# A fixed order of steps up to chunk 3, chunk 0's relu outputs kept in DRAM, and early keys and values summed by TensorE

## The chip, the cores and the metric

The kernel runs on one core of a Trainium2 chip. The metric is the device time of one execution, in microseconds (us). TensorE (PE; PEld is its weight load), VectorE (DVE), ScalarE (ACT), GpSimd (POOL) and the DMA queues, most of them issued by SyncE (SP), each work through their own list of instructions in order and wait for each other by semaphores.

## The reference

Attention over keys and values that are averaged in groups of eight along the sequence, then a layer norm, a two-layer network with relu, and the sum of both. The weights come as 64-bit floats, all else as 32-bit.

```python
# q, k, v: 8 batches x 8 heads x 576 rows x 64
k_p = k.reshape(B, H, 72, 8, 64).mean(axis=3)
v_p = v.reshape(B, H, 72, 8, 64).mean(axis=3)
attn = softmax(q @ k_p.T / sqrt(64))
x = (attn @ v_p), heads side by side           # 8 x 576 x 512
xn = (x - mean) / sqrt(var + 1e-6) * g_ln
out = x + relu(xn @ w_ch1) @ w_ch2             # 512 -> 2048 -> 512
```

## The kernel before

The 4608 rows are 36 tiles of 128, and nine chunks of four tiles (0 to 8). A tile goes through two stages. `stage_a` loads the tile's queries, forms the scores with the block-diagonal pooled keys `kblk` (TensorE, L310), takes their maximum and subtracts it (VectorE, L319 and L320), takes the exponential (ScalarE, L329) and transposes the result: the first five tiles (`XT`) by TensorE (L335), copied out by ScalarE (L336), the others by a DMA from a float16 pair `phl` (ScalarE L338, GpSimd L345 and L348, SP L355). `values` multiplies with the pooled values (L392, L394, L395), divides by the sums (VectorE L399 to L409, ScalarE L416), normalises (VectorE L420 to L425 with an iterated inverse square root, L372 and L375; ScalarE L428) and transposes z for the network: by TensorE for the first tiles (L438 to L440), for later ones as a float16 pair and a DMA transpose.

Every float32 matrix product of the network is three products of float16 halves. The first layer of chunks 0 and 1 is `ffn_in` (L625), whose relu goes to a ring tile in two halves, by ScalarE (L633) and VectorE (L634); from chunk 2 on it is `slot`, 28 Strassen products of twelve matmuls (L551). The second layer is `ffn_out` (L655): eight groups of 24 matmuls in a chunk, two for each tile, each evicted by VectorE (L665).

The weights have to be made first. Each of eight blocks of w1 and of w2 (1 MB of 64-bit floats) is loaded, converted to float32 (`convert`: ScalarE L189, VectorE L198 or GpSimd, VectorE L199, ScalarE L207 with the block's maximum), and then split into two float16 parts by `split_w` (ScalarE L164, VectorE L165), once the maxima of four blocks have given the scale. The first half of the first layer needs the four splits of blocks 0 to 3, and the first group of the second layer those of four blocks of w2. `w_forms` prepares sums of w1's blocks for the Strassen products on GpSimd (L510, L513).

Keys and values are pooled in halves of a batch: on VectorE by one reduction (L682, L690), or on GpSimd by three additions (L248 to L252, L260 to L262). Values of batch 0 are summed by TensorE, with a band of ones (L755); its keys by VectorE and GpSimd. From batch 1 on, values are then split into a float16 pair, which four DMAs on ScalarE's queue lay out (L283, L284).

The order is set twice. The table `START` names operations up to the end of chunk 1 (`R.1.2` loads block 2 of w1, `C` converts, `S` splits, `A.4` and `B.4` are the two stages of tile 4, `I.0.2` is the first layer of chunk 0 for relu quarter 2, `O.0.1` the second half of its second layer, `HK` and `HV` are halves of pooling). It is emitted operation by operation, and then a scheduler that simulates a timeline reorders instructions within each engine's list. From chunk 2 on a loop emits 28 products and eight groups of the second layer, numbered 0 to 35, and puts the two stages of the next chunk's tiles ahead of the numbers in `A_AT` and `B_AT`; the same scheduler orders it.

Of the kernel before, what the change touches and what calls it, by code (L numbers as in the profile page):

```python
# [70 lines left out]
def attn_ffn_kernel(ctx: ExitStack, tc: tile.TileContext, qT, vn, kT, v, g, w1, w2, out):  # L71
# [74 lines left out]
    def all_max(src, n=P):  # L146


        e, dst = scalar_tile("rowmax"), scalar_tile("allmax")
# [9 lines left out]
        nc.vector.tensor_reduce(out=dst, in_=ps, axis=AX.X, op=ALU.max)
        return dst  # L160

    def split(src, scale, hi, lo):

        nc.scalar.activation(out=hi, in_=src, func=AF.Copy, scale=scale)  # L164
        nc.vector.scalar_tensor_tensor(  # L165
# [16 lines left out]
    def convert(mat, b, on_pool=0):  # L182
# [6 lines left out]
        nc.scalar.activation(  # L189
            out=w, in_=hi.bitcast(F32), func=AF.Prelu, scale=2.0**-112, alpha=-(2.0**32)  # L190
        )
# [7 lines left out]
        nc.vector.scalar_tensor_tensor(  # L199
            out=w.bitcast(I32),  # L200
            in0=w.bitcast(I32),
# [5 lines left out]
        nc.scalar.activation(  # L207
# [37 lines left out]
    def pool_k(b, p, eng):

        kr = kraw.pop((b, p))
        eng.tensor_add(out=kr[:, 0:4, :], in0=kr[:, 0:4, :], in1=kr[:, 4:8, :])  # L248
# [579 lines left out]
```

## Time and profile before

| | |
|---|---|
| three runs | 858.0, 860.56 and 857.74 us; median 858.0 |
| the profiled execution | 858.18 us, of which the span 856.5 us |
| mean granted clock of TensorE | 0.976 |
| instructions | 14301 |
| last matmul of the second layer, chunk 1, 2, 3 | 255.2, 351.4, 435.6 us |
| the same, chunk 4 to 8 | 520.9, 605.1, 690.35, 774.5, 852.6 us |

The times of the trace count from the start of the span. A row of the timeline gives the start, the length, the engine, the line, the operation with output and inputs, the number of instructions in the row, and in brackets the idle time ahead of it with what ended it. From chunk 3 on a chunk takes 84.2 to 85.3 us; chunk 2 took 96.2 us, and the first two together 255.2 us.

### The profile page before, as it was taken

How to read it: one execution, taken by the hardware profiler on the slowest of the kernel's cores; microseconds unless marked ns; L12 is line 12 of the kernel's file. 1: busy time of each engine (PE TensorE's matmuls, PEld its weight loads, DVE VectorE, ACT ScalarE, POOL GpSimd, SP SyncE). 2: the span in 40 equal slices, each digit the busy share in tenths (PEclk: the TensorE clock that was granted, in tenths of full speed). 3: DMA queues.
4: the chain of work that ended last, by engine and by line, in shares of the span. 5: the costliest groups of instructions: out<-in, count | busy, mean ns of one | idle time of the engine just before them, and what ended most of it. 6: DMA issues, size and time to landing. Idle time of an engine off the chain costs nothing.

```text
span 856.5 us, 14301 instructions
## 1 busy us (share of the span) xinstructions
PE 811.7 (95%) x5601; PEld 526.3 (61%) x5601; DVE 530.3 (62%) x1168; ACT 361.4 (42%) x705; POOL 226.3 (26%) x238
## 2 busy tenths in 40 slices
PE   5587989999998899999999999999999999999998
PEld 3466644444546764796478647954785479548743
DVE  5899899124885588387837853785457545843421
ACT  4788653234334543364335523552354235423300
POOL 2586391992212111121210230113011201220000
PEclk9768999999998999999999999999999999999999
DMA  9978352200747144354334451334133512440001
GB/s 336 363 282 275 81 131 82 75 1 16 159 118 173 49 85 90 99 142 84 83 81 102 103 106 38 88 79 103 38 74 75 99 41 47 63 99 25 1 1 50
DMA packets 142867, 86.39 MB, mean 101 GB/s; under 512 B 121824, under 2 KB 122832, under 8 KB 140752
## 3 DMA queue, kind: packets, MB, share of 16 engines
q1 hardware_dynamic: 141456, 84.43, 38.3%
q10 hardware_dynamic: 1344, 1.05, 0.6%
q8 instruction: 44, 0.72, 0.3%
q14 instruction: 23, 0.19, 0.1%
HBM read 45.09 MB, written 9.44 MB: 64 GB/s over the span
## 4 chain that ended last, share of the span: by engine, by line
PE 74%; DVE 11%; DMA 6%; ACT 3%; POOL 3%; issue 2%; SPq 1%; DVEq 0%; POOLq 0%; ACTq 0%
PE ps_f L655 34%; PE ps_f L551 28%; PE ps_f L625 6%; PE ps L310 3%; DMA vr<-in_v_dram 2%; DVE vp L690 2%; DVE w L165 2%; DMA pt<-phl 2%; DVE w L199 1%; POOL w L510 1%; PE ps L394 1%; DVE kp L682 1%; PE ps L395 1%; DMA kr<-in_kT_dram 1%; DMA zz<-hl 1%
## 5 line engine op out<-in xcount | busy, mean ns | idle before, releaser
L655 PE MATMUL ps_f<-w,ring 128*128 128x512 f16 x1728 | 381.6, 380 | 3.4 <-DVE ring L634 2.0
L655 PEld LDWEIGHTS <-ring 128*128 128x128 f16 x1728 | 167.5, 98 | 199.1 <-issue 5.7
L551 PE MATMUL ps_f<-zz,w 128*128 128x256 f16 x1344 | 164.0, 274 | 6.5 <-DMA zz<-hl 4.5
L551 PEld LDWEIGHTS <-w 128*128 128x128 f16 x1344 | 131.6, 98 | 26.0 <-issue 7.7
L551 PE MATMUL ps_f<-zz,raw 128*128 128x256 f16 x1008 | 121.7, 273 | 1.4 <-DMA zz<-hl 0.8
L345 POOL TENSOR_TENSOR phl<-e,phl 128x512 f16<-128x512 f32 x31 | 37.1, 1195 | 324.7 <-ACT phl L338 315.6
L665 DVE SCALAR_TENSOR_TENSOR x<-ps_f,c_out,x 128x512 f32<-128x512 f32 x72 | 53.5, 745 | 109.6 <-PE ps_f L655 109.6
L551 PEld LDWEIGHTS <-raw 128*128 128x128 f16 x1008 | 98.3, 98 | 14.4 <-issue 2.2
L625 PE MATMUL ps_f<-zz,w 128*128 128x512 f16 (+1 forms) x480 | 89.9, 348 | 6.4 <-DVE ring L634 5.5
L625 PEld LDWEIGHTS <-w 128*128 128x128 f16 x480 | 48.4, 102 | 45.0 <-issue 7.2
L571 DVE SCALAR_TENSOR_TENSOR ring<-ps_f,ring 128x512 f16<-128x512 f32 x56 | 38.4, 685 | 31.2 <-ACT ring L570 31.1
L310 PE MATMUL ps<-kblk,q 128*128 128x144 f32 (+1 forms) x320 | 49.3, 309 | 8.2 <-DVE raw L248 7.7
L582 ACT COPY w<-ps_f 128x512 f32<-128x512 f32 x28 | 16.2, 579 | 93.6 <-PE ps_f L551 93.6
L428 ACT ACTIVATE z<-x,nb,y 128x512 f32<-128x512 f32 x36 | 29.2, 814 | 54.5 <-DVE nb L425 41.8
L571 DVE SCALAR_TENSOR_TENSOR ring<-v,ring 128x512 f16<-128x512 f32 x56 | 40.7, 728 | 16.2 <-ACT ring L570 15.6
L310 PEld LDWEIGHTS ps<-kblk,q 128*128 128x128 f32 (+1 forms) x320 | 41.7, 195 | 12.6 <-DVE raw L248 7.7
L690 DVE TENSOR_REDUCE vp<-vr 72x64 f32<-72x512 f32 x44 | 44.6, 1025 | 7.4 <-DMA vr<-in_v_dram 7.0
L416 ACT ACTIVATE x<-ps,rs 128x64 f32<-128x64 f32 x144 | 33.3, 313 | 31.5 <-DVE x L409 20.8
L570 ACT ACTIVATE ring<-v 128x512 f16<-128x512 f32 x56 | 35.1, 627 | 20.2 <-DVE v L593 13.1
L634 DVE SCALAR_TENSOR_TENSOR ring<-ps_f,ring 128x512 f16<-128x512 f32 (+1 forms) x40 | 22.4, 579 | 32.8 <-ACT ring L633 32.7
L338 ACT CAST phl<-e 128x1024 f16<-128x1024 f32 x31 | 32.4, 1044 | 20.0 <-DMA pt<-phl 18.5
L329 ACT ACTIVATE e<-e 128x576 f32<-128x576 f32 x36 | 24.6, 683 | 37.0 <-DVE e L320 36.7
(125 smaller groups left out, 932.4 us busy)
## 6 DMA issues: line engine op xcount, KB each, us to landing
raw<-in_w_dram SPq DMA_DIRECT2D x12, 1024.0 KB
q<-in_qT_dram SPq DMA_DIRECT2D x36, 256.0 KB
out_dram<-x SPq DMA_DIRECT2D x36, 256.0 KB
kr<-in_kT_dram SPq DMA_DIRECT2D x29, 288.0 KB
vr<-in_v_dram SPq DMA_DIRECT2D x56, 144.0 KB
ring<-in_w_dram SPq DMA_DIRECT2D x4, 1024.0 KB
raw<-in_vn_dram SPq DMA_DIRECT2D x1, 1024.0 KB
va<-vh ACTq DMA_DIRECT2D x14, 65.0 KB
```

The source lines that it names most:

```text
L310: nc.tensor.matmul(ps[r, p // 2, p % 2 * 2 * KV : (p % 2 + 1) * 2 * KV], lhsT=q[:, p, r], rhs=kblk[b % NKB][:, p, :], start=True, stop=True,)
L338: nc.scalar.copy(out=ph[:, :, :, 0:KA], in_=e[:, :, 0:KA].unsqueeze(1).broadcast_to([P, 2, H, KA]))
L345: nc.gpsimd.tensor_tensor(out=ph[:, 0, :, KA:P], in0=e[:, :, 0:KA], in1=ph[:, 0, :, 0:KA], op=ALU.subtract)
L416: nc.scalar.activation(out=xh[:, 4 + i, :], in_=px[:, 1, i, 0:D], func=AF.Copy, scale=rs[:, 4 + i : 5 + i])
L428: nc.scalar.activation(out=z, in_=x, func=AF.Identity, scale=y, bias=nb)
L551: nc.tensor.matmul(ps[:, j], lhsT=w_form(wb, int(m == 2), k)[:, fs], rhs=z_form(za, int(m == 1), k), start=(first and i == 0 and j == 0), ...
L570: nc.scalar.activation(out=hi, in_=src, func=AF.Relu)
L571: nc.vector.scalar_tensor_tensor(out=lo, in0=src, scalar=0.0, in1=hi, op0=ALU.max, op1=ALU.subtract)
L625: nc.tensor.matmul(ps, lhsT=w[:, part, fs], rhs=zT[:, kz, cols], start=(n == 0), stop=(n == 3 * NKT - 1),)
L655: nc.tensor.matmul(ps, lhsT=h[:, part, i, cols], rhs=w[:, wp, j], start=(n == 0), stop=(n == 3 * NFT // 2 - 1),)
L665: nc.vector.scalar_tensor_tensor(out=x, in0=ps, scalar=c_out[:, half : half + 1], in1=x, op0=ALU.mult, op1=ALU.add)
L690: nc.vector.tensor_reduce(out=vp[b][:, h, 0:D], in_=vraw.pop((b, h)).rearrange("p l d -> p d l"), axis=AX.X, op=ALU.add,)
```

## The change

Line numbers below are those of the changed code where a row has a new number: L208 and L210 are the two halves of a split (before L164 and L165), L236, L246, L248 and L257 the conversion (L189, L198, L199, L207), L698 and L730 the first and second layer (L625, L655), L707 and L709 the relu (L633, L634), L761 and L770 the reductions (L682, L690), L741 the eviction of the second layer (L665).

*A fixed order.* Every operation becomes a generator that gives up control after each step. `START` names a step by naming its operation once more, now up to the end of chunk 2 (`U.2.1.3` is product 3 of group 1), and the table is run inside a manual schedule: on each engine the instructions stand as written. The loop starts at chunk 3, still under the scheduler, with other numbers in `A_AT` and `B_AT`.

*Relu outputs in DRAM.* `X.q` stores relu quarter q of chunk 0 (1 MB) to DRAM and `Y.q` loads it back into a ring tile, both on SP's queue.

*Pooling.* Keys and values of batches 0 and 1 are loaded in natural layout into room that is free then (tiles of w2, z's second half) and summed by TensorE: keys by twenty small matmuls a batch (`pe_k`), copied to `kblk` by ScalarE (L842); values by five (`pe_v`), copied by ScalarE (L853). Values of batch 1 on are still split as before. All other pooling is one reduction on VectorE, over eight neighbouring elements, since k and v are laid out with those innermost; GpSimd pools nothing.

*Conversion.* `convert` may put its intermediate into PSUM.

```diff
-A_AT, B_AT = (6, 13, 20, 26), (28, 29, 30, 31)
+A_AT, B_AT = (12, 20, 28, 30), (27, 29, 31, 33)
 START = """
-LK Q.0 R.1.2 Q.1 R.1.7 LV C.1.2 R.1.1 C.1.1.1 V0 G R.1.0 HK.1.0 K0 Q.2 R.2.0 C.1.0 R.1.5 A.0 R.1.3
...
+Q.0 LK.0 R.1.6 LV.0 Q.1 LV.1 R.1.2 R.2.4 Q.3 R.1.0 G K.0 R.1.3 R.1.5 LK.1 K.0 HV.2.0 HV.2.1 HK.3.1 K.0 R.1.1
...
+I.0.1.1 C.2.1.1 I.0.1.1 I.0.1.1 C.2.5.0.1 I.0.0.1 S.1.7 M2.0 A.4 I.0.0.1 I.0.1.1 S.1.7 M2.0 C.2.5.0.1 I.0.2 X.0
+A.4 M2.0 T.0.0.1 I.0.1.1 S.2.0 A.5 X.1 B.4 I.0.2 S.2.0 A.5 T.0.0.1 I.0.3 B.4 B.4 I.0.2 Y.0 S.2.1 B.4 I.0.2 A.5
...
     def split(src, scale, hi, lo):
         nc.scalar.activation(out=hi, in_=src, func=AF.Copy, scale=scale)
+        yield
         nc.vector.scalar_tensor_tensor(
...
-    def convert(mat, b, on_pool=0):
+    def convert(mat, b, on_pool=0, in_psum=0):
...
-        w = w_f32(mat, b)
+        w = u = w_f32(mat, b)
+        if in_psum:
+            u = ps_2.tile([P, 2, 512], F32, name="ps_2").rearrange("p a n -> p (a n)")
...
-        kraw[b, p] = kr = wk2.tile([P, POOL, KV], F32, name="kr") if kr is None else kr
+        kraw[b, p] = kr = wk2.tile([P, KV, POOL], F32, name="kr")
...
-        vraw[b, h] = vr = wk2.tile([KV, POOL, D], F32, name="vr") if vr is None else vr
+        vraw[b, h] = vr = wk2.tile([KV, D, POOL], F32, name="vr")
...
         nc.vector.tensor_reduce(
-            out=kp, in_=kr.rearrange("p l k -> p k l"), axis=AX.X, op=ALU.add
+            out=kp, in_=kr, axis=AX.X, op=ALU.add
...
+    def spare(i):
+        if i == 3:
+            kr = wk2.tile([P, KV, POOL], F32, name="kr").rearrange("p k l -> p (k l)")
+            return zz[:, 1].rearrange("p k n -> p (k n)").bitcast(F32), kr
+        return (wt[2][:, 3 * i : 3 * i + 3].rearrange("p s a n -> p (s a n)").bitcast(F32),)
...
+    def pe_k(b):
+        ps = ps_f.tile([P, CH], F32, name="ps_f")[:, : NPAIR * KV].rearrange("p (a k) -> p a k", k=KV)
+        for r, x in enumerate(stage.pop(("k", b))):
+            n = x.shape[0]
+            c = slice(r * P // POOL, r * P // POOL + n // POOL)
+            for p in range(NPAIR):
+                nc.tensor.matmul(
+                    ps[:, p, c],
+                    lhsT=x[:, p * P : (p + 1) * P],
+                    rhs=ones[:n, : n // POOL],
+                    start=True,
+                    stop=True,
+                )
+            yield
+        for j in range(2):
+            r, c = slice(j * D, (j + 1) * D), slice(j * KV, (j + 1) * KV)
+            nc.scalar.copy(out=kblk[b % NKB][r, :, c], in_=ps[r])
+
+    def pe_v(b):
         ps = ps_f.tile([P, CH], F32, name="ps_f")[:KV]
+        for r, x in enumerate(stage.pop(("v", b))):
+            w = pool_w[: x.shape[0], D - r * P // POOL :][:, :KV]
+            nc.tensor.matmul(ps, lhsT=w, rhs=x, start=(r == 0), stop=(r == NRT - 1))
+            yield
...
+    def put_h(q):
+        hd[q] = dram.tile([P, 2, FPQ, CH], F16, name=f"hd{q}")
+        nc.sync.dma_start(out=hd[q], in_=hT.pop((0, q)))
+
+    def get_h(q):
+        hT[0, q] = ring_tile()
+        nc.sync.dma_start(out=hT[0, q], in_=hd.pop(q))
...
+    def step(token):
+        if token not in begun:
+            name, *args = token.split(".")
+            begun[token] = iter(ops[name](*map(int, args)) or ())
+        next(begun[token], None)
+
+    with tc.manual_schedule():
+        for token in START.split():
+            step(token)
+
-    for c in range(ST, NRUN):
+    for c in range(ST + 1, NRUN):
...
-        "kT": k.reshape(B, NPAIR, 2, KV, POOL, D).transpose(0, 2, 5, 1, 4, 3).reshape(B, P, NPAIR, POOL, KV),
+        "kT": k.reshape(B, NPAIR, 2, KV, POOL, D).transpose(0, 2, 5, 1, 3, 4).reshape(B, P, NPAIR, KV, POOL),
```

The order moves at three places. The first is ScalarE's list around the last of the four splits that the first layer waits for; before it read (tiles w_85 and raw hold w1, w_86 w2):

```order
L164 ACTIVATE w_85<-w_85,gs 128x1024
L336 COPY pt<-ps_410 72x1024
L189 ACTIVATE w_85<-raw 128x1024
L164 ACTIVATE w_85<-w_85,gs 128x1024
L207 ACTIVATE raw,wm_92<-w_85 128x1024
L189 ACTIVATE w_85<-raw 128x1024
L164 ACTIVATE w_85<-w_85,gs 128x1024
L416 ACTIVATE x<-ps_591,rs 128x64 x4
L207 ACTIVATE raw,wm_92<-w_85 128x1024
L164 ACTIVATE w_85<-w_85,gs 128x1024
```

and now, with w_87 for w1 and w_88 for w2:

```order
L208 ACTIVATE w_87<-w_87,gs 128x1024
L368 ACTIVATE e<-e 128x576
L236 ACTIVATE w_87<-raw 128x1024
L257 ACTIVATE raw,wm_95<-w_88 128x1024
L377 COPY pt<-ps_532 72x1024
L208 ACTIVATE w_87<-w_87,gs 128x1024
L257 ACTIVATE raw,wm_94<-w_87 128x1024
L208 ACTIVATE w_87<-w_87,gs 128x1024
L461 ACTIVATE x<-ps_555,rs 128x64 x4
L368 ACTIVATE e<-e 128x576
L236 ACTIVATE ps_586<-raw 128x1024
L208 ACTIVATE w_87<-w_87,gs 128x1024
```

The four splits stand in twelve rows instead of ten, with two exponentials and one conversion of w2 between them; ahead of them now stand the values of three tiles instead of two, and the split and the laying out of batch 1's values.

The second is SP's list behind the last weight loads, where the relu quarters go out (hd are the DRAM tiles) and come back:

```order
L225 DMA raw<-in_w_dram 128x2048 x4
L873 DMA hd_950<-ring 128x4096
L873 DMA hd_964<-ring 128x4096
L877 DMA ring<-hd_950 128x4096
L398 DMA_TRANSPOSE pt<-phl_105 128x16x128
L877 DMA ring<-hd_964 128x4096
```

Between two quarters stands the transpose (L398, before L355) of the probabilities of tile 5; before, that transpose had only loads ahead of it on SP.

The third is VectorE's list around the splits of w2 that the first group of the second layer waits for. Before, between the second split and the fourth:

```order
L165 SCALAR_TENSOR_TENSOR w_86<-w_86,ws 128x1024
L375 TENSOR_SCALAR y<-a,y 128x1
L634 SCALAR_TENSOR_TENSOR ring<-ps_f,ring 128x512
L372 TENSOR_SCALAR a<-y,ve 128x1
L159 TENSOR_REDUCE allmax<-ps_f 128x1
L690 TENSOR_REDUCE vp<-vr 72x64
L399 TENSOR_SCALAR sm<-ps_1294,cv 128x8
```

and now:

```order
L210 SCALAR_TENSOR_TENSOR w_88<-w_88,ws 128x1024
L357 TENSOR_REDUCE mx<-ps_1057 128x8
L246 TENSOR_SCALAR raw<-raw 128x1024
L490 TENSOR_TENSOR zz<-ps_f,zz 128x4x128
L709 SCALAR_TENSOR_TENSOR ring<-ps_f,ring 128x512 x2
L210 SCALAR_TENSOR_TENSOR w_88<-w_88,ws 128x1024
L359 TENSOR_TENSOR e<-ps_1057,mx 128x576
L357 TENSOR_REDUCE mx<-ps_1118 128x8
L210 SCALAR_TENSOR_TENSOR w_88<-w_88,ws 128x1024
```

The reductions of values (L690) that stood between the splits are now few, and scores of tiles 6 and 7 (L357, L359) stand there.

More of the change, by code (lines that the diff above doesn't have):

```diff
@@ L422, in values @@
         y = rsqrt(mv[:, 1:2])
-        Z[t] = z = wk2.tile([P, DM], F32, name="z")
         nb = scalar_tile("nb")
@@ L674, in stage_a @@
             load_q(t + 2)
-        scores(t)
-        probs(t)
+            yield
+        yield from scores(t)
+        yield
+        yield from probs(t)
     def reduce_k(b, p):
@@ L726, in attn_ffn_kernel, with half_k, half_v, load_rows @@
+            yield
+        if i == H - 1:
+            yield from max_v(b)
+            yield from split_v(b)
+    def half_k(b, i):
+        yield from prep_k(b, (2 * i, 2 * i + 1))
+    def half_v(b, i):
+        yield from prep_v(b, range(4 * i, 4 * i + 4))
     stage = {}
[L728 removed]
+    def load_rows(name, src, at, rest=None):
         full = (NRT - 1) * P
[L730 to L732 removed]
+        a = at[:, : full // P * DM].rearrange("p (r d) -> p r d", d=DM)
+        rest = at[:, full // P * DM :] if rest is None else rest
+        rest = rest[: S - full, :DM]
@@ L733, in load_rows @@
         nc.sync.dma_start(out=a, in_=src[:full].rearrange("(r p) d -> p r d", p=P))
         nc.sync.dma_start(out=rest, in_=src[full:])
-        stage[name] = [(a[:, r], pool_w[:, D - r * P // POOL :][:, :KV]) for r in range(NRT - 1)]
-        r = NRT - 1
-        stage[name].append((rest, pool_w[: S - full, D - r * P // POOL :][:, :KV]))
-    def first_loads():
-        kr = raw_tile().rearrange("p a f c -> p (a f c)").bitcast(F32)
-        kr = kr[:, : 3 * POOL * KV].rearrange("p (a l k) -> p a l k", l=POOL, k=KV)
-        load_k(0, 3)
-        for p in range(3):
-            load_k(0, p, kr[:, p])
@@ L746, in first_k @@
-    def first_k():
-        pool_k(0, 3, nc.gpsimd)
-        for p in range(3):
-            pool_k(0, p, nc.vector)
-    def first_v():
-        ps = ps_f.tile([P, CH], F32, name="ps_f")[:KV]
-        rows = stage.pop("v")
-        for i, (x, w) in enumerate(rows):
-            nc.tensor.matmul(ps, lhsT=w, rhs=x, start=(i == 0), stop=(i == NRT - 1))
-        vp[0] = wk2.tile([KV, H, D + 1], F32, name="vp")
-        nc.vector.memset(vp[0][:, :, D:], float(POOL))
-        nc.scalar.copy(out=vp[0][:, :, 0:D], in_=ps.rearrange("p (h d) -> p h d", d=D))
@@ L760, in load_vn, with rows_k, rows_v @@
-    def load_vn():
-        load_rows("v", vn)
+        stage[name] = [a[:, r] for r in range(NRT - 1)] + [rest]
+    def spare(i):
[3 more added lines that the diff above has]
+        return (wt[2][:, 3 * i : 3 * i + 3].rearrange("p s a n -> p (s a n)").bitcast(F32),)
+    def rows_k(b):
+        load_rows(("k", b), kn[b], *spare(2 * b))
+    def rows_v(b):
+        load_rows(("v", b), vn[b], *spare(2 * b + 1))
@@ new lines, in pe_v @@
+    def pe_v(b):
+        ps = ps_f.tile([P, CH], F32, name="ps_f")[:KV]
+        for r, x in enumerate(stage.pop(("v", b))):
+            w = pool_w[: x.shape[0], D - r * P // POOL :][:, :KV]
+            nc.tensor.matmul(ps, lhsT=w, rhs=x, start=(r == 0), stop=(r == NRT - 1))
+            yield
+        vp[b] = wk2.tile([KV, H, D + 1], F32, name="vp")
+        if b < 2:
+            nc.vector.memset(vp[b][:, :, D:], float(POOL))
+        nc.scalar.copy(out=vp[b][:, :, 0:D], in_=ps.rearrange("p (h d) -> p h d", d=D))
+        if b:
+            yield
+            yield from max_v(b)
+            yield from split_v(b)
```

220 lines of the change are left out of this document (143 added, 77 removed).

## The prediction

> **What bounds the kernel now.** I began with the share of each engine over the span and the chain of waits, then cut the span into stages. The first fence has the two lines of the page; the second has one row for each stage (start and end; its length; busy time and instructions of PE, PEld, DVE, ACT and POOL; granted clock; DMA share; GB/s).
>
> ```profile
> PE 811.7 (95%) x5601; PEld 526.3 (61%) x5601; DVE 530.3 (62%) x1168; ACT 361.4 (42%) x705; POOL 226.3 (26%) x238
> PE 74%; DVE 11%; DMA 6%; ACT 3%; POOL 3%; issue 2%; SPq 1%; DVEq 0%; POOLq 0%; ACTq 0%
> ```
>
> ```profile
> 10.10:57.00 46.90, 33.72 (x166) 26.16 (x166) 37.92 (x71) 38.23 (x60) 24.75 (x32) 0.75 0.95 343
> 57.00:82.90 25.90, 17.89 (x135) 13.57 (x133) 25.79 (x65) 20.89 (x41) 19.66 (x26) 0.87 0.84 289
> 82.90:121.60 38.70, 36.65 (x284) 23.41 (x284) 33.91 (x71) 24.44 (x49) 23.73 (x26) 1.00 0.45 109
> 121.60:260.20 138.60, 132.00 (x670) 62.34 (x670) 85.20 (x196) 47.37 (x85) 65.46 (x45) 0.98 0.32 80
> 260.20:351.40 91.20, 87.78 (x647) 59.12 (x648) 58.99 (x129) 37.06 (x78) 16.64 (x19) 0.97 0.45 96
> 351.40:852.60 501.20, 501.20 (x3700) 339.73 (x3697) 282.59 (x616) 191.82 (x395) 72.69 (x80) 1.00 0.32 71
> ```
>
> From 351.4 us TensorE has no gap (501.20 of 501.20): an edit there can only lose, or remove matmuls. Idle TensorE time is nearly all ahead of 121.6. There the trace names VectorE: 25.79 of 25.90 us busy in the second row, 33.91 of 38.70 in the third, while ACT and POOL have slack. The timeline of TensorE shows what the first 121 us are for:
>
> ```profile
> 48.78 1.91 PE L625 MATMUL ps_f<-zz,w 128*128 128x256 f16 x8
> 67.28 6.91 PE L625 MATMUL ps_f<-zz,w 128*128 128x256 f16 x48 [5.48 <-DVE ring L634]
> 121.57 3.14 PE L655 MATMUL ps_f<-w,ring 128*128 128x512 f16 x7 [2.05 <-DVE ring L634]
> 126.09 4.26 PE L655 MATMUL ps_f<-w,ring 128*128 128x512 f16 x19 [1.38 <-DVE w L165]
> 166.49 41.61 PE L625 MATMUL ps_f<-zz,w 128*128 128x512 f16 x192 [0.31 <-DMA zz<-hl]
> 260.20 2.72 PE L551 MATMUL ps_f<-zz,w 128*128 128x256 f16 x12 [4.51 <-DMA zz<-hl]
> 748.42 26.06 PE L655 MATMUL ps_f<-w,ring 128*128 128x512 f16 x120
> ```
>
> The first layer of chunk 0 trickles from 48.78 (L625), waits 5.48 us for VectorE's half of a relu (L634), and the second layer (L655) starts at 121.57, with waits for VectorE's relu and for its split of w2 (L165). So there are three milestones to price: the fourth w1 split (the first group of the first layer needs four), the start of the second layer, and the start of chunk 2 at 260.20.
>
> **The change, term by term.** *Term 1, to the fourth w1 split.* ACT starts it, DVE finishes it:
>
> ```profile
> 10.13 1.12 ACT L189 ACTIVATE w<-ring 128x1024 f32<-128x1024 f32 x1 [7.74 <-DMA ring<-in_w_dram]
> 55.86 1.15 ACT L164 ACTIVATE w<-w,gs 128x1024 f16<-128x1024 f32 x1
> 58.60 1.27 DVE L165 SCALAR_TENSOR_TENSOR w<-w,gs 128x1024 f16<-128x1024 f32 x1
> ```
>
> It ends at 58.60 + 1.27 = 59.9. Ahead of it the new order of ACT has one conversion step fewer (L207) and more of other things; the group rows with their means (ns):
>
> ```profile
> L207 ACT ACTIVATE raw<-w 128x1024 f32<-128x1024 f32 x12 | 13.7, 1147 | 5.4 <-DVE w L199 5.4
> L416 ACT ACTIVATE x<-ps,rs 128x64 f32<-128x64 f32 x144 | 33.3, 313 | 31.5 <-DVE x L409 20.8 <-DVE vh L276 6.9 <-issue 3.7
> L329 ACT ACTIVATE e<-e 128x576 f32<-128x576 f32 x36 | 24.6, 683 | 37.0 <-DVE e L320 36.7
> L428 ACT ACTIVATE z<-x,nb,y 128x512 f32<-128x512 f32 x36 | 29.2, 814 | 54.5 <-DVE nb L425 41.8 <-DVE y L363 9.1 <-DVE ve L360 3.6
> L319 DVE TENSOR_REDUCE mx<-ps 128x8 f32<-128x576 f32 x36 | 27.1, 753 | 16.7 <-PE ps L310 16.7
> L372 DVE TENSOR_SCALAR a<-y,ve 128x1 f32<-128x1 f32 x108 | 28.9, 268 | 2.0
> L248 DVE TENSOR_TENSOR raw<-raw 128x288 f32<-128x288 f32 x3 | 1.4, 457 | 2.2 <-DMA raw<-in_kT_dram 2.2
> L682 DVE TENSOR_REDUCE kp<-kr 128x72 f32<-128x576 f32 x20 | 23.8, 1192 | 4.9 <-DMA kr<-in_kT_dram 2.6 <-ACT kblk L687 2.2
> L690 DVE TENSOR_REDUCE vp<-vr 72x64 f32<-72x512 f32 x44 | 44.6, 1025 | 7.4 <-DMA vr<-in_v_dram 7.0
> L755 PE MATMUL ps_f<-raw,pool_w 128*72 128x512 f32 x8 | 4.8, 755 | 0.0
> ```
>
> ```profile
> 83.14 0.52 ACTq L283 DMA_DIRECT2D va<-vh  x1
> 85.51 0.67 ACTq L284 DMA_DIRECT2D vb<-vh  x1
> ```
>
> ACT: four more of L416 (1.25), one L329 (0.68), one L428 (0.81), one more copy of transposed z (0.6, estimated at near L329), four copies of pooled keys out of PSUM (1.7, estimated at half a L428 each), one more V copy and the V split of batch 1 (1.3), less one L207 (1.15): +5.2. The four DMA issues that belong to a V split now come ahead too; before they held ACT's queue from 83.14 to 86.2: +3, in all +8. DVE: the sums of batch 0's keys go (twelve additions, three at 0.457 and the others at 0.2 to 0.4: 3.8), and one conversion and one maximum (2.2); in come one tile's scores (twice 0.75, L319's size), one more normalisation with six further steps of its square root at 0.27 and 0.2 (4.5), one residual (0.7) and the V work (1.5): +2.9 with small ones. If the waits between them stay, DVE alone gives 59.9 + 2.9 = 62.8, ACT 59.9 + 8 = 67.9. The edit also puts pooling matmuls in front: ten for V cost 4.8 + 1.1 before; now twenty for V and two groups of twenty small ones for K, at most 5 us a group by L755's mean. Lower bound 58 (the new work hides in waits and some waits shrink), upper 73 (both groups in series with the first tile's scores). I take **65**, between the two engines.
>
> *Term 2, from there to the second layer.* Before: 121.6 − 59.9 = 61.7. TensorE's own work in that stretch is now 192 half-width matmuls (6.91/48 = 0.144 us each with its start-up; 0.113 in the dense run from 82.88, 5.07/45), 84 of full width at 41.61/192 = 0.217 and about 7 us of attention: 21.7 + 18.2 + 7 = 46.9.
>
> ```profile
> 82.88 5.07 PE L625 MATMUL ps_f<-zz,w 128*128 128x256 f16 x45 [0.24 <-DVE zz L440]
> 117.03 3.70 DVE L165 SCALAR_TENSOR_TENSOR w<-w,ws 128x1024 f16<-128x1024 f32 x1
> 117.49 2.13 POOL L510 TENSOR_TENSOR w<-w 128x1024 f32<-128x1024 f16 x1
> ```
>
> What went on besides in that stretch before was the pooling of batches 1 to 3: L690 and L682 on DVE and POOL's sums, of which most leave the stretch (batches 0 and 1 are pooled by TensorE; batch 2 and 3 come later). What DVE must do there in the new order adds to 44 to 48 us, at the means of the same lines. In the two rows of before it was busy 59.70 of 64.60, 92%: 47/0.92 = 51. So the term is **51**, set by DVE rather than by TensorE's 46.9; bounds 47 and 60.
>
> A split of DVE that met a POOL subtraction took 3.70 us instead of 1.27: it began at 117.03, POOL's L510 ended at 119.62, and the split 1.1 us after it. The Trainium skill ("SBUF — State Buffer", section "SBUF: two separate sides") calls this an exclusive lock: a DVE instruction with two SBUF inputs and a POOL one block each other for a whole instruction. The trace agrees, with 2.4 us lost. By this rule the new order would be hurt where POOL's sums of weights stand beside the eight splits of w2; what that would cost is the second rival.
>
> The new store and load of each relu quarter moves 1.05 MB out and back; at the first stage's 343 GB/s that is 6.1 us. Seven groups of the first layer stand between (84 × 0.217 = 18 us), so I put it at nothing; without that cover it costs 6 us once. The Trainium skill ("DMA: Bandwidth & Descriptors", section "Anatomy of one DMA — SWDGE (gpsimd) path") fits a transfer with 2 us and bytes at 436 GB/s, for another kind of queue; by that the round trip would be an estimated 8.8 us, still under 18, and the sum is unchanged. SP waits at the store for the quarter's last relu, and behind it on SP's queue wait the transposed probabilities of tile 5, for which TensorE's values of that tile would wait.
>
> *Term 3, second layer of chunk 0 to chunk 2.* Before 138.6 with 132.0 busy. Counted in the order, twelve full-width matmuls (2.6) and attention of two more pieces (2) come in, so 136.6; the 4.51 us wait for transposed z at 260.20 should shrink, because chunk 2's tiles now start beside the second layer of chunk 1. I allow 2.4 of stalls: **139**; bounds 136.6 and 147.
>
> *Term 4, chunk 2.* 28 products of twelve matmuls at 775.63 − 774.33 = 1.30 us (the next fence), 192 matmuls at 0.217 and 7.6 of attention are 86; before it took 91.2. With 2.5 of stalls **88.5** (86 to 95).
>
> *Term 5, chunks 3 to 8.* Scheduled as before but for the two tables of places. Values of the next chunk's last tile now come later, so that fewer matmuls cover the way from values to transposed z. The chain of before, in the boundary at 774:
>
> ```profile
> 748.39 0.20 PE L395 MATMUL ps<-vb,pt 88*128 88x65 f16 x1
> ...
> 774.33 1.47 PE L551 MATMUL ps_f<-zz,w 128*128 128x256 f16 x12
> 775.63 2.78 PE L551 MATMUL ps_f<-zz,raw 128*128 128x256 f16 x24
> ...
> 755.55 0.21 DVE L425 TENSOR_SCALAR nb<-mv,y 128x1 f32<-128x1 f32 x1
> 761.86 3.14 SPq L475 DMA_TRANSPOSE zz<-hl  x1
> ```
>
> From the last value matmul (748.6) to the issue of the transpose is 13.3 us and to its landing 17.5 to 18 (the transpose's own row has 3.14 of queue; I add 4.5 from the issue). The new order of DVE has the same links with one eviction between, as here. The cover was 26.06 (120 matmuls); now it is 72 × 0.217 = 15.7 plus a product and a score tile, 17.8. So a wait of 0 to 2 us at each of five boundaries: I take 0.5 each, 2.5, less 1 for the tile already done: **502.7** (500 to 511). The DVE reductions read their inner eight elements in line instead of at a stride; they become shorter (L690 takes 1025 ns where a reduction of the same size without stride, L266, takes 674), but DVE is only 282.59 of 501.20 busy there: nothing.
>
> ```profile
> L266 DVE TENSOR_REDUCE mv<-vp 72x1 f32<-72x512 f32 x7 | 4.7, 674 | 0.0
> ```
>
> Sum: 65 + 51 + 139 + 88.5 + 502.7 + 3.9 (what follows 852.6) = 850.1 of span. The profiled execution took 1.7 us more than its span of 856.5, and 858.18 lies on the median of 858.0: 851.8, about **852 us**.
>
> **Rivals.** *R1, the gain is larger.* The new order takes the waits out of the head as well: 61 for term 1, 47 for term 2 (TensorE's own), 137, 86 and 501 behind: 835.9, so 838. For it: DVE's list is only 2.9 us longer up to the split. Against: every wait would have to go. 0.20.
>
> *R2, slower: DVE and POOL lock each other in the head.* In a fixed order an engine cannot take a later instruction that is ready. POOL has nine or ten instructions of 2.13 us in term 2, DVE twelve splits and four conversions with two SBUF inputs; if half meet and lose 1.5 us, that is 12, and TensorE's clock falls as in the first row (0.75): 68 + 63 + 143 = 274 instead of 255, so 867 with the rest less smooth. It decides once the second layer starts after 122. For it: the 3.70 us row; against: before had the same instructions in 38.7 us. 0.15.
>
> *R3, the boundaries wait.* 2 us at five of them instead of 0.5, and 2 at chunk 3: 861. The cover of 17.8 against 17.5 speaks for it; against, that a wait of 2 needs another delay. 0.10.
>
> *R4, the change does not do what its name says.* In TensorE's order chunk 1's first layer still stands behind chunk 0's second, so the trip to DRAM frees nothing and is only a wait: 6 us at each of two halves if the cover is gone, 858 to 864; taken with a head that is no earlier. 0.10.
>
> **How the numbers follow.** Forecast (845 to 858) 0.45, R1 0.20, R2 0.15, R3 0.10, R4 0.10. What can be told from no change is 0.3%, 2.6 us: faster is below 855.4, slower above 860.6. Forecast gives 0.38 faster, 0.06 same; R1 0.20 faster; R2 0.15 slower; R3 and R4 together 0.04 faster, 0.11 same, 0.05 slower: 0.62, 0.17, 0.21 after rounding. The range 838 to 864 reaches R1 and the milder part of R2.
>
> **What would show it.** Right: the fourth w1 split near 65, the second layer starting near 116 with VectorE at over 90% in between, chunk 2 starting near 255 and no wait over 1 us at a boundary. Wrong: a start of the second layer after 122 with long DVE splits beside POOL (R2); a wait on the reloaded quarters (R4); waits for transposed z of 2 us (R3); a start before 110 (R1).

## The result, and the profile after

The changed kernel took 854.5 us (median of 13 runs, 852.0 to 857.5), beside 860.6 us of the kernel before on the same chip: ratio 0.9934, 95% interval 0.9914 to 0.9953. It is faster by 0.5 to 0.9%. The forecast was 852 us and faster. Its profiled execution is the slowest of its runs, 857.5 us with a span of 855.7, so the two spans lie only 0.8 us apart; the ratio counts, and the spans are used to see where time went.

The windows by stage of the changed kernel, cut at its own milestones (columns as in the prediction's second fence):

```profile
10.10:57.00 46.90, 45.21 (x212) 35.93 (x214) 33.09 (x85) 30.90 (x53) 3.38 (x3) 0.79 0.94 336
57.00:71.30 14.30, 9.07 (x59) 6.93 (x55) 13.60 (x26) 13.70 (x21) 0.00 (x0) 0.74 0.53 187
71.30:116.50 45.20, 45.18 (x331) 32.38 (x332) 42.09 (x78) 34.90 (x60) 19.51 (x10) 0.96 0.62 213
116.50:252.60 136.10, 136.07 (x745) 66.47 (x744) 108.11 (x232) 58.41 (x114) 59.22 (x39) 1.00 0.55 144
252.60:343.20 90.60, 87.24 (x652) 58.56 (x651) 56.62 (x134) 37.69 (x79) 18.00 (x21) 0.98 0.51 112
343.20:851.80 508.60, 502.26 (x3691) 340.50 (x3688) 282.51 (x614) 194.21 (x392) 70.13 (x78) 1.00 0.31 67
```

And TensorE's timeline at the milestones:

```profile
71.32 5.75 PE L698 MATMUL ps_f<-zz,w 128*128 128x256 f16 x37 [1.27 <-DVE w L210]
116.52 5.34 PE L730 MATMUL ps_f<-w,ring 128*128 128x512 f16 x24
252.55 8.02 PE L619 MATMUL ps_f<-zz,w 128*128 128x256 f16 x72
431.94 3.34 PE L619 MATMUL ps_f<-zz,raw 128*128 128x256 f16 x19 [3.48 <-DMA zz<-hl]
```

The fourth w1 split now ends 11.4 us later than before (71.3 against 59.9), and from there TensorE works without a gap: 45.18 of 45.20 us up to the second layer, 136.07 of 136.10 up to chunk 2. The second layer starts 5 us earlier than before, chunk 2 is done 8 us earlier (343.2 against 351.4). Then the gain is given back: chunks 3 to 8 took 501.20 us without a gap before, now 508.60, with waits for transposed z. So in this execution the head gains 8 and the loop loses 7.

| term | forecast | measured |
|---|---|---|
| to the fourth w1 split | 65 | 71.3 |
| to the second layer | 51 | 45.2 |
| to chunk 2 | 139 | 136.1 |
| chunk 2 | 88.5 | 90.6 |
| chunks 3 to 8 | 502.7 | 508.6 |
| behind the last matmul | 3.9 | 3.9 |

### The profile page after: what moved, and what is told of

Read it like the earlier page. It is cut to its first block, busy times and chain, and to the rows that moved or that the text cites. A ratio compares the mean times of both kernels' runs of the same rounds, so it can differ in the third digit from the quotient of the medians.

```text
span 855.7 us, 14396 instructions
## 1 busy us (share of the span) xinstructions
PE 827.4 (97%) x5691; PEld 543.2 (63%) x5691; DVE 538.2 (63%) x1170; ACT 371.4 (43%) x718; POOL 171.6 (20%) x160
## 5 line engine op out<-in xcount | busy, mean ns | idle before, releaser
L730 PE MATMUL ps_f<-w,ring 128*128 128x512 f16 x1728 | 382.4, 380 | 2.6 <-DVE ring L640 2.6
L730 PEld LDWEIGHTS <-ring 128*128 128x128 f16 x1728 | 167.7, 98 | 198.1 <-DVE ring L640 2.8
L619 PEld LDWEIGHTS <-w 128*128 128x128 f16 x1344 | 130.7, 98 | 18.4
L619 PE MATMUL ps_f<-zz,raw 128*128 128x256 f16 x1008 | 124.1, 274 | 7.1 <-DMA zz<-hl 7.1
L741 DVE SCALAR_TENSOR_TENSOR x<-ps_f,c_out,x 128x512 f32<-128x512 f32 x72 | 53.7, 746 | 83.8 <-PE ps_f L730 82.7
L698 PE MATMUL ps_f<-zz,w 128*128 128x512 f16 (+1 forms) x480 | 87.7, 344 | 1.5 <-DVE w L210 1.3
L698 PEld LDWEIGHTS <-w 128*128 128x128 f16 x480 | 47.9, 101 | 38.6 <-DVE w L210 1.7
L640 DVE SCALAR_TENSOR_TENSOR ring<-ps_f,ring 128x512 f16<-128x512 f32 x56 | 38.4, 686 | 28.4 <-ACT ring L638 27.9
L640 DVE SCALAR_TENSOR_TENSOR ring<-v,ring 128x512 f16<-128x512 f32 x56 | 39.0, 697 | 16.0 <-ACT ring L638 13.8
L461 ACT ACTIVATE x<-ps,rs 128x64 f32<-128x64 f32 x144 | 33.2, 311 | 35.6 <-DVE x L453 31.7
L347 PE MATMUL ps<-kblk,q 128*128 128x144 f32 (+1 forms) x320 | 45.8, 304 | 1.0 <-DVE e L359 1.0
L638 ACT ACTIVATE ring<-ps_f 128x512 f16<-128x512 f32 x56 | 33.3, 595 | 24.0 <-PE ps_f L619 21.3
L770 DVE TENSOR_REDUCE vp<-vr 72x64 f32<-72x512 f32 x48 | 32.0, 676 | 16.5 <-DMA vr<-in_v_dram 16.5
L654 DVE TENSOR_TENSOR w<-ps_f,w 128x512 f32<-128x512 f32 x28 | 19.3, 688 | 32.9 <-PE ps_f L619 29.2
```

The source lines that it names most:

```text
L347: nc.tensor.matmul(ps[r, p // 2, p % 2 * 2 * KV : (p % 2 + 1) * 2 * KV], lhsT=q[:, p, r], rhs=kblk[b % NKB][:, p, :], start=True, stop=True,)
L461: nc.scalar.activation(out=xh[:, 4 + i, :], in_=px[:, 1, i, 0:D], func=AF.Copy, scale=rs[:, 4 + i : 5 + i])
L619: nc.tensor.matmul(ps[:, j], lhsT=w_form(wb, int(m == 2), k)[:, fs], rhs=z_form(za, int(m == 1), k), start=(first and i == 0 and j == 0), ...
L638: nc.scalar.activation(out=hi, in_=src, func=AF.Relu)
L640: nc.vector.scalar_tensor_tensor(out=lo, in0=src, scalar=0.0, in1=hi, op0=ALU.max, op1=ALU.subtract)
L698: nc.tensor.matmul(ps, lhsT=w[:, part, fs], rhs=zT[:, kz, cols], start=(n == 0), stop=(n == 3 * NKT - 1),)
```

## The experiments

For each kernel the ratio is to the kernel before, in runs on the same chip. "The loop" is the time from the end of chunk 2 to the last matmul in the profile.

| kernel | ratio (95% interval) | second layer starts | the loop |
|---|---|---|---|
| before | 1 | 121.6 | 501.2 |
| changed | 0.9934 (0.9914 to 0.9953) | 116.5 | 508.6 |
| changed, once more | 0.9912 (0.9878 to 0.9946) | 116.8 | 508.0 |
| changed, old places | 0.9837 (0.9816 to 0.9857) | 117.2 | 500.2 |
| before, new places | 1.0034 (1.0021 to 1.0048) | 124.8 | 504.2 |
| no trip to DRAM | 0.9935 (0.9919 to 0.9952) | 114.9 | 508.0 |
| same table, scheduled | 1.0208 (1.0186 to 1.0230) | 141.5 | 506.9 |
| keys on VectorE | 0.9817 (0.9784 to 0.9850) | 114.5 | 501.7 |
| keys on VectorE, old places | 0.9825 (0.9792 to 0.9858) | 113.2 | 500.2 |
| quarters loaded twice | 1.0036 (1.0014 to 1.0058) | 117.8 | 504.1 |
| batch 1's keys on VectorE | 0.9870 (0.9842 to 0.9897) | 119.4 | 501.3 |
| old places of values only | 0.9858 (0.9827 to 0.9888) | 116.9 | 500.8 |
| old places of scores only | 0.9898 (0.9868 to 0.9928) | 115.3 | 506.1 |
| keys on VectorE, old places, no trip | 0.9828 (0.9789 to 0.9866) | 113.5 | 500.2 |

### The places in the loop

```diff
-A_AT, B_AT = (12, 20, 28, 30), (27, 29, 31, 33)
+A_AT, B_AT = (6, 13, 20, 26), (28, 29, 30, 31)
```

> The changed kernel with the loop's two tables of places as before: A_AT (6, 13, 20, 26) and B_AT (28, 29, 30, 31); the fixed order up to chunk 2 is untouched. Theory (the later places cost the waits for transposed z at the boundaries, 6.3 us in the profiled execution of the changed kernel, where only 2.5 were expected): these waits go, the head stays (second layer of chunk 0 from 116.5, chunk 2 from 252.6), and the time falls by 5 to 6 us, to about 849, ratio to before about 0.987. Rival (the boundary waits are covered time that comes back elsewhere, since the earlier scores now stand among the products of the first half of a chunk and hold up evictions there): no change against the changed kernel, ratio 0.993, with new waits of TensorE for ScalarE or VectorE within the chunks.

The window from the end of chunk 2 to the last matmul of this kernel, and TensorE's total wait for transposed z over the whole execution (waited in all, times, longest), then the same total of the changed kernel:

```profile
344.20:844.50 500.30, 500.26 (x3692) 338.76 (x3689) 273.36 (x615) 190.11 (x392) 72.34 (x78) 1.00 0.30 68
```

```profile
PE ps_f L619 <- DMA zz<-hl: 0.8, 1, 0.8
```

```profile
PE ps_f L619 <- DMA zz<-hl: 7.1, 5, 3.5
```

The one wait left lies in chunk 2, ahead of the loop; of the five of the changed kernel, four lie in the loop, 6.3 us in all. The ratio fell by 1.0%, more than the 0.6 to 0.7% expected, and the loop by 8 us. The rival, that the time would come back as other waits, is out: TensorE is busy 500.26 of 500.30.

The four waits are 6.3 us of these 8; the other 2 are busy time (502.26 us in the changed kernel). Behind its longest wait, which ends at 431.94, TensorE's granted clock is 0.61 in one stretch of 4 us, and 24 matmuls pass in it where 37 pass in the next (columns as above; the clock is the third number from the end, 1.00 is full speed):

```profile
432.00:436.00 4.00, 4.00 (x24) 3.02 (x25) 0.69 (x1) 0.59 (x1) 0.00 (x0) 0.61 0.00 0
436.00:440.00 4.00, 4.00 (x37) 3.51 (x36) 0.69 (x1) 1.13 (x2) 0.00 (x0) 0.96 0.00 0
```

So a long wait can cost more than its length. It need not: a wait of 3.04 us in the kernel without the trip to DRAM has a clock of 1.00 behind it (430 to 434 us).

The same tables put into the kernel before:

```diff
-A_AT, B_AT = (6, 13, 20, 26), (28, 29, 30, 31)
+A_AT, B_AT = (12, 20, 28, 30), (27, 29, 31, 33)
```

> The kernel before with only the tables of places of the changed kernel, A_AT (12, 20, 28, 30) and B_AT (27, 29, 31, 33). Theory (the places alone make the boundaries wait): slower by 4 to 7 us, ratio 1.005 to 1.008, with waits for transposed z at the ends of chunks that were free of them. Rival (the waits belong to the changed kernel's VectorE list, which the scheduler orders otherwise there): ratio 1.000 and no such waits.

The direction is the theory's, the size is less: 0.3%, the loop 3 us longer, with waits for z of 0.64, 1.42 and 0.60 us. The head, which the edit does not name, also ends 1.7 us later (353.2 against 351.4). The places cost time in either kernel, but more in the changed one.

Which of the two tables it is:

```diff
-A_AT, B_AT = (12, 20, 28, 30), (27, 29, 31, 33)
+A_AT, B_AT = (12, 20, 28, 30), (28, 29, 30, 31)   # the one kernel
+A_AT, B_AT = (6, 13, 20, 26), (27, 29, 31, 33)    # the other
```

> The changed kernel with B_AT (28, 29, 30, 31) as before and A_AT (12, 20, 28, 30) as changed; in TensorE's list 82 to 90 matmuls of the second layer then stand behind the last values of a chunk instead of 72 and a product. Theory (the cover behind the last values decides): 18 to 19.5 us of cover, the waits for transposed z under 1 us in all, ratio 0.984 to 0.987. Rival (the places of scores decide, since the late scores crowd VectorE's list ahead of the boundary): 0.992 to 0.994.

> The changed kernel with A_AT (6, 13, 20, 26) as before and B_AT (27, 29, 31, 33) as changed; the cover behind the last values is again 72 matmuls and a product. Theory (the cover decides): waits for transposed z as in the changed kernel, ratio 0.990 to 0.995. Rival (the places of scores decide): no waits, 0.984.

TensorE's first wait for z in the loop of the kernel with the old places of values, and of the one with the old places of scores:

```profile
427.70 2.79 PE L619 MATMUL ps_f<-zz,raw 128*128 128x256 f16 x24 [0.60 <-DMA zz<-hl]
```

```profile
430.51 3.12 PE L619 MATMUL ps_f<-zz,raw 128*128 128x256 f16 x19 [2.97 <-DMA zz<-hl]
```

With the values back in their places the loop takes 500.8 us, with only the scores back 506.1, with both 500.2. So of some 8 us the places of the values are worth 6 to 8, and those of the scores less than 3. The intervals of the two ratios overlap, so the verdict rests on the loops.

### The DRAM trip

The table without its eight steps X and Y:

```diff
-... C.2.5.0.1 I.0.2 X.0
-A.4 M2.0 T.0.0.1 I.0.1.1 S.2.0 A.5 X.1 B.4 ...
+... C.2.5.0.1 I.0.2
+A.4 M2.0 T.0.0.1 I.0.1.1 S.2.0 A.5 B.4 ...
```

> The changed kernel without the eight steps X and Y: chunk 0's relu quarters stay in their ring tiles, and TensorE reads them from there. Theory (the store and load are hidden, 18 us of first layer stand between): the same time as the changed kernel within 1 us, ratio 0.993, second layer of chunk 0 still from 116.5. Rival 1 (the trip is a wait, since SP's queue holds the transposed probabilities behind it): 3 to 6 us faster, ratio 0.986 to 0.990. Rival 2 (the trip frees ring tiles that something needs early): slower by several us, ratio near 1.

No difference: 0.9935 against 0.9934. The second layer starts at 114.9 here; the five kernels with the changed kernel's own head start it between 115.3 and 117.2, so a microsecond or two there may be the trip's. By the ratio it costs nothing and brings nothing. Making it longer:

```diff
-        nc.sync.dma_start(out=hT[0, q], in_=hd.pop(q))
+        nc.sync.dma_start(out=hT[0, q], in_=hd[q])
+        nc.sync.dma_start(out=hT[0, q], in_=hd.pop(q))
```

> The changed kernel with each relu quarter loaded back twice into the same ring tile, one load behind the other, so that the trip to DRAM is longer by one transfer of 1 MB (about 3 to 5 us) for each quarter. Theory (the trip has more cover than it needs: leaving it out changed nothing): no difference, ratio 0.993, second layer of chunk 0 from 116.5 to 117.5. Rival (it just fits): the second layer's first group waits for the ring, 2 to 5 us, ratio 0.996 to 0.999.

This cost 1.0%, twice what the rival had. TensorE's rows with a wait between 117 and 165 us, then, ahead of the longest of them, SP's rows for the third quarter (L877 and L878 are the two loads) and VectorE's wait:

```profile
123.22 4.45 PE L730 MATMUL ps_f<-w,ring 128*128 128x512 f16 x12 [2.71 <-DMA ring<-hd]
148.18 2.29 PE L347 MATMUL ps<-kblk,q 128*128 128x144 f32 x8 [6.29 <-ACT x L461]
160.30 2.76 PE L730 MATMUL ps_f<-w,ring 128*128 128x512 f16 x12 [1.56 <-DMA ring<-hd]
```

```profile
132.33 0.37 SPq L877 DMA_DIRECT2D ring<-hd  x1
138.78 0.34 SPq L878 DMA_DIRECT2D ring<-hd  x1
139.22 0.78 SPq L297 DMA_DIRECT2D vr<-in_v_dram  x2
145.59 0.68 DVE L770 TENSOR_REDUCE vp<-vr 72x64 f32<-72x512 f32 x1 [6.76 <-DMA vr<-in_v_dram]
```

The waits sum to 10.6 us; TensorE's busy time from the second layer to chunk 2 grows by 3.8 us besides (139.8 against 136.1), at a granted clock of 0.92 up to 180 us. Two waits are for the ring itself. The longest is not. Attention waits for ScalarE (L461), ScalarE for VectorE, and VectorE's list stands still for 6.76 us until values have been loaded. SP issues the last loads of values ahead of that moment at 139.22, right behind the second load of the quarter, which it issues 6.5 us behind the first (132.33, then 138.78). The edit lengthens the trip by about 6 us a quarter and TensorE waits 2.7 and 1.6 us for the ring, so the trip has some 3 to 4 us to spare there; what stands behind it on SP's list can have less.

### The fixed order

```diff
-    with tc.manual_schedule():
-        for token in START.split():
-            step(token)
+    for token in START.split():
+        step(token)
```

> The changed kernel with the same table of steps, but emitted under the scheduler instead of the manual schedule, so that the order within each engine's list is the scheduler's again; pooling, DRAM trip and places are those of the changed kernel. Theory (the gain of the head is less work on VectorE and GpSimd there, not the fixed order as such): second layer of chunk 0 within 3 us of 116.5, time within 3 us of the changed kernel, ratio 0.992 to 0.997. Rival (the fixed order is what brings the gain): the second layer starts near 121 as before, ratio 0.998 to 1.003.

Both theories fall short: the same table under the scheduler is 2.1% slower than the kernel before, and 2.8% slower than with the fixed order. Against the fixed order all of it lies ahead of the second layer, which starts at 141.5, 25 us later; at the end of chunk 2 it is 22.5 us (365.7 against 343.2), and the loop is 1.7 us shorter. Two windows, and ScalarE's first w1 split, in the scheduled kernel:

```profile
10.10:57.00 46.90, 42.00 (x192) 32.17 (x191) 27.11 (x52) 27.12 (x43) 4.41 (x3) 0.79 0.91 329
75.60:141.50 65.90, 53.97 (x399) 37.52 (x400) 59.56 (x131) 47.87 (x87) 22.56 (x14) 0.90 0.58 177
```

```profile
74.37 1.16 ACT L208 ACTIVATE w<-w,gs 128x1024 f16<-128x1024 f32 x1
```

Up to 57 us VectorE does 27.11 us of work where the fixed order has 33.09, and ScalarE 27.12 where it has 30.90; what was left undone stands between 75.6 and 141.5, where VectorE is busy 59.56 us instead of the 42.09 that the fixed order leaves to that stretch, and TensorE has gaps of 12 us. So this table needs the fixed order. Why the scheduler chose so for it was not looked into. A fixed order for the table of before was not tried, nor was what each other part of the change (pooling by one reduction, the intermediate of a conversion in PSUM) is worth in the head.

### Keys by TensorE or by VectorE

```diff
     def rows_k(b):
-        load_rows(("k", b), kn[b], *spare(2 * b))
+        x = spare(2 * b)[0][:, : NPAIR * KV * POOL].rearrange("p (a k l) -> p a k l", a=NPAIR, k=KV)
+        nc.sync.dma_start(out=x, in_=kT[b])
+        stage["k", b] = x
...
     def pe_k(b):
-        for r, x in enumerate(stage.pop(("k", b))):
...
-                nc.tensor.matmul(
...
+        x = stage.pop(("k", b))
+        for p in range(NPAIR):
+            nc.vector.tensor_reduce(out=ps[:, p], in_=x[:, p], axis=AX.X, op=ALU.add)
             yield
```

> The changed kernel with the keys of batches 0 and 1 loaded as the later batches' and summed by four VectorE reductions each into the same PSUM tile, in the place of twenty small matmuls; all else, places included, as in the changed kernel. In its profile the two groups of matmuls took 8.78 and 8.79 us of TensorE, and TensorE was busy 45.21 of the 46.90 us from 10.1 to 57. Theory (TensorE's cold small matmuls hold up the head: scores of tile 0 wait for them until 18.2): scores start 5 to 7 us earlier, the fourth w1 split ends 5 to 8 us earlier than 71.3, the second layer starts near 110, and the time falls by 4 to 7 us, ratio 0.985 to 0.989. Rival (VectorE and ScalarE set the fourth split, their lists are as long as before): the split ends within 2 us of 71.3 and the time stays, ratio 0.993.

The time fell by 1.2% against the changed kernel, more than expected, but not for the reason given. The window, what TensorE then waits for, and four rows up to the fourth split (the last):

```profile
10.10:57.00 46.90, 29.74 (x146) 20.10 (x148) 36.85 (x90) 30.30 (x54) 3.33 (x3) 0.81 0.87 328
```

```profile
PE ps_f L486 <- ACT z L475: 8.1, 2, 7.7
PE ps_f L195 <- DVE rowmax L173: 4.3, 1, 4.3
```

```profile
20.28 1.20 ACT L236 ACTIVATE w<-ring 128x1024 f32<-128x1024 f32 x1 [1.11 <-DMA ring<-in_w_dram]
43.84 0.72 ACT L208 ACTIVATE vh<-vp,sv 72x512 f16<-72x512 f32 x1
46.71 1.55 DVE L832 TENSOR_REDUCE ps_f<-w 128x72 f32<-128x576 f32 x2
67.77 1.16 ACT L208 ACTIVATE w<-w,gs 128x1024 f16<-128x1024 f32 x1
```

TensorE's 45.21 us of that stretch become 29.74, and it spends them waiting for ScalarE and VectorE; the fourth split begins at 67.77 instead of 68.23 (the changed kernel's rows are shown below, under term 1). So the rival's forecast for the split came true, but the matmuls were not free: without them ScalarE was 2.6 us ahead at the split of batch 1's values (43.84 against 46.40), but after the two reductions that VectorE makes in their place at 46.71 only 0.5 us of that remained. The edit exchanges one delay for another and does not price the matmuls alone. Some 4 us are won up to the end of chunk 2 (339.2 against 343.2), and 7 in the loop, where the table of places and each engine's list are the same as in the changed kernel; 5 of the 7 are waits for z (1.3 us against 6.3) and 2 are busy time, the clock's share shown above. Where the two loops part, ahead of the first boundary, VectorE's last reduction of values and SP's transpose of z, first in the changed kernel, then with keys on VectorE:

```profile
405.78 0.68 DVE L770 TENSOR_REDUCE vp<-vr 72x64 f32<-72x512 f32 x1 [2.46 <-DMA vr<-in_v_dram]
...
426.05 3.86 SPq L533 DMA_TRANSPOSE zz<-hl  x1
```

```profile
400.17 0.68 DVE L770 TENSOR_REDUCE vp<-vr 72x64 f32<-72x512 f32 x1 [0.69 <-DMA vr<-in_v_dram]
...
420.44 3.08 SPq L533 DMA_TRANSPOSE zz<-hl  x1
```

VectorE stands still for its load 1.8 us longer, and with it the chain to z; the transpose's row is another 0.8 us longer. With so little cover both reach TensorE. With the old places nothing of that is left to win:

```diff
 # keys on VectorE as above, and
-A_AT, B_AT = (12, 20, 28, 30), (27, 29, 31, 33)
+A_AT, B_AT = (6, 13, 20, 26), (28, 29, 30, 31)
```

> The same with the tables of places as before. The places alone brought the ratio from 0.9934 to 0.9837. Theory (two separate causes, head and boundaries): the gains add, ratio 0.976 to 0.980, about 842. Rival (keys on VectorE bring nothing): 0.984.

The gains do not add: 0.9825 against 0.9817 with the new places, since most of what the old places win had been won. With batch 1 alone on VectorE (the same edit for b = 1):

> The changed kernel with only batch 1's keys on VectorE, batch 0's by TensorE as in the change. Theory (both groups of small matmuls hold up TensorE at 0.44 us each, and the second stands just ahead of the transposes of z and the scores that the first layer needs): about half of the gain of moving both, 2 to 4 us, ratio 0.988 to 0.991. Rival 1 (only the first group matters, since it delays the first scores): no gain, 0.993. Rival 2 (only the second matters): all of it.

0.9870, half of the gain, as expected, but again in the loop (501.3) and not in the head, where the second layer even starts at 119.4. And the changed kernel once more, to see whether its waits come again:

> The changed kernel itself once more, beside the next three and with a profile of its own. In three profiles with the loop's places as changed the waits for transposed z came to 6.3 to 7.9 us with keys by TensorE and 1.3 to 2.7 us with keys on VectorE, though every engine's list in the loop is the same. Theory (the cover of 17.8 us is so near to the chain that the landing of single loads of values decides, and which way differs between executions): ratio 0.990 to 0.996, waits for z anywhere from 1 to 8 us. Rival (the keys on TensorE bring the waits about): again 6 to 8 us of waits.

They do: 5.8 us in three waits, 3.8 the longest, at three of the four boundaries of the first profile. This is within what the theory of chance allowed (1 to 8 us) and just under the rival's 6; that it comes at the same boundaries speaks for the rival, but one repeat does not decide it. With keys of batch 1 on TensorE and the new places of values, the loop took 504.1 to 508.6 us in six profiles, with them on VectorE 501.3 and 501.7. What carries an edit of the first 57 us into loads at 400 us was not found. The kernels differ in the number of transfers issued before. Eight fewer (no trip) left the loop at 508.0, four more (quarters loaded twice) went with 504.1, so an edit that leaves the keys alone moved the loop too; whether it is the number or the moments was not tried.

All three together:

```diff
 # keys on VectorE and the old places as above, and no steps X and Y
```

> Keys of batches 0 and 1 on VectorE, the tables of places as before, and no trip of chunk 0's relu quarters to DRAM. Theory (the trip changes nothing, the others are what e6 has): within 1 us of that kernel, ratio 0.980 to 0.984. Rival (with a faster head the trip becomes a wait): 0.976 to 0.979.

0.9828, the same as without the trip's removal. The fastest kernels measured are those with keys on VectorE, 1.7 to 1.8% below the kernel before; the changed kernel with nothing but its two tables put back stands at 1.6%, and the intervals overlap.

## Why the prediction was right or wrong, point by point

*Time and direction* were right, 852 for 854.5, and that is partly luck. In the profiled execution terms 1, 4 and 5 were too low by 6.3, 2.1 and 5.9 us and terms 2 and 3 too high by 5.8 and 2.9, so that 8.7 of 14.3 us cancelled.

*Term 1 (65; 71.3)* was too low. The step that failed is the sum: I added the new work of each list to the old end, with the waits as they were, and took 65 between ScalarE's 67.9 and VectorE's 62.8. The delay came from the start of the chain, which I had not priced. The scale needs the maxima of blocks 0 to 3 of w1, the ring tiles. The first of these began its conversion at 10.13 us before (the prediction shows the row). Now block 6 and the values of two batches are loaded ahead of it, and on ScalarE's list its conversion stands behind tile 0's exponential, whose scores wait for the key sums on TensorE:

```profile
20.23 0.76 DVE L357 TENSOR_REDUCE mx<-ps 128x8 f32<-128x576 f32 x1 [7.02 <-PE ps L347]
21.81 0.68 ACT L368 ACTIVATE e<-e 128x576 f32<-128x576 f32 x1 [4.46 <-DVE e L359]
22.40 1.15 ACT L236 ACTIVATE w<-ring 128x1024 f32<-128x1024 f32 x1
46.40 0.72 ACT L208 ACTIVATE vh<-vp,sv 72x512 f16<-72x512 f32 x1
49.88 1.22 DVE L248 SCALAR_TENSOR_TENSOR w<-ps,ring 128x1024 int32<-128x1024 int32 x1
51.98 1.14 ACT L257 ACTIVATE ring<-w 128x1024 f32<-128x1024 f32 x1 [2.36 <-DMA vb<-vh]
57.18 1.15 ACT L208 ACTIVATE w<-w,gs 128x1024 f16<-128x1024 f32 x1
68.23 1.16 ACT L208 ACTIVATE w<-w,gs 128x1024 f16<-128x1024 f32 x1
```

The conversion at 22.40 is 12.3 us later than before, the first split (57.18 against 46.30) 10.9, the fourth (68.23 against 55.86) 12.4. How much of this is the loads and how much the scores was not tried; with keys on VectorE the exponential came at 18.49 and the conversion then waited for its load until 20.28. The term that I had named, four DMA issues of batch 1's values at 3 us, cost less than 1: they end just ahead of the last maximum (L257 at 51.98), whose input VectorE delivers only at 51.1 (49.88 and 1.22). I had also put the key matmuls at no more than 5 us a group; they took 8.78 and 8.79. The upper bound of 73, with the groups in series with the first scores, was the better reading.

*Term 2 (51; 45.2)* was too high. I had put VectorE's work at 47 us and divided by the share of before, 92%; it had 42.09 us of work and was 93% busy. By that share the measured work would have given 45.8, so the rows do not refute the rule, only its sum. TensorE had no gap, 45.18 of 45.20 us, and its own work was the term; my 46.9 for it was right to 2 us.

*The lock of VectorE and GpSimd (R2)* did not reach TensorE. The splits of w2, before and now (ns: least, median, most), and one of GpSimd's instructions now:

```profile
L165 DVE SCALAR_TENSOR_TENSOR w<-w,ws x8: 1248/1274/3703, 117.0 to 148.0; 128x1024 f16<-128x1024 f32 x8
```

```profile
L210 DVE SCALAR_TENSOR_TENSOR w<-w,ws x8: 1270/1512/2059, 98.5 to 139.7; 128x1024 f16<-128x1024 f32 x8
107.71 3.04 POOL L568 TENSOR_TENSOR raw<-w,raw 128x1024 f16<-128x1024 f32 x1 [3.51 <-ACT raw L575]
```

The longest split is 2.06 us instead of 3.70, but the median is longer, 1.51 instead of 1.27, with more of GpSimd's 2.13 us instructions around them, and some of those now take up to 3.04. This does not contradict the rule of the Trainium skill ("SBUF — State Buffer", section "SBUF: two separate sides") by which one of the two blocks the other for a whole instruction. The loss is spread in smaller pieces over both engines, and from 71.3 us to chunk 2 TensorE waits for none of them.

*The DRAM trip* at nothing was right, as its removal shows. The price behind it was not: I gave the trip 6.1 us under a cover of 18. SP's rows in the changed kernel show the first two quarters from 93.91 to a last load issued at 105.28, with the transpose between them:

```profile
93.91 4.07 SPq L873 DMA_DIRECT2D hd<-ring  x2
98.59 0.32 SPq L877 DMA_DIRECT2D ring<-hd  x1
102.14 3.09 SPq L398 DMA_TRANSPOSE pt<-phl  x1
105.28 0.57 SPq L877 DMA_DIRECT2D ring<-hd  x1
```

That is 11.4 us to the last issue alone for two quarters, ahead of a second layer at 116.5. R4 was right that the trip buys nothing, and wrong that it costs.

*Terms 3 and 4* held within 3 us. The wait of 4.51 us ahead of chunk 2 is gone, as said; 2.6 us in chunk 2 wait for a relu (L640) that I had only under stalls.

*Term 5 (502.7; 508.6)* named the right mechanism, chain against cover, 17.5 to 18 us against 17.8, and mis-sized the chain. At the first boundary where it waits, it took 21.1 us from the last value matmul to the products that read z (410.87 to 431.94) instead of 17.5 to 18: 15.2 instead of 13.3 to the issue of the transpose, since VectorE's list came late out of its 2.46 us wait for a load, and 5.9 instead of 4.5 from there. No row of the prediction has the 4.5. With keys on VectorE the same two are 13.5 and 4.9, 18.4 in all, and the wait is 0.79. So I took 0.5 us a boundary, and the loop lost 7 to 8 with the new places, 2 of them by the clock behind the longest wait. R3, given 0.10, is what happened, beside a larger gain of the head. I had read a margin of nothing as a small loss: VectorE's list also holds reductions that wait for loads, which I had put at nothing because VectorE was half idle.

## What to carry to other kernels

Where a chain and its cover come out equal on paper, take the loss as the spread of the loads in the chain, not as the difference; a few matmuls more behind the last values were worth 0.5 to 0.8% here. In an order written by hand, follow the chain from the first load through every engine to the event that counts, waits included; adding each engine's new work to the old end missed 6 us. And test a new order without its companions: here the tables of places took back more than half of what the head had won, and the trip to DRAM did nothing.

## What the runs showed of the hardware

A group of twenty float32 matmuls with 16 or 8 columns took 8.8 us, each as two instructions; the second group ran at a granted clock of 0.50 (43.4 to 52.2 us). By these rows, which leave out those with 8 columns, the weight loads took as long as the products:

```profile
L832 PE MATMUL ps_f<-pool_w,w 128*128 128x16 f32 x64 | 14.0, 374 | 7.7 <-DMA w<-in_kn_dram 7.7
L832 PEld LDWEIGHTS ps_f<-pool_w,w 128*128 128x128 f32 x64 | 13.8, 332 | 7.7 <-issue 7.7
```

The reduction over eight neighbouring elements took 676 ns for the values (L770) where the strided one had 1025, and 743 for the keys (L761) where it had 1192. A wait of TensorE of 3.48 us was followed by a granted clock of 0.61 in a stretch of 4 us. And 7 us of the loop could depend on an edit 340 us earlier that left every engine's list in the loop as it was; that was not expected, and is not explained.
